# A fused attention and MoE kernel: batch 0 in two query parts (384, 192) with a MoE span for each, and a new order of the early loads

## The chip, the cores and the metric

The kernel runs on one core of one Trainium2 chip. The metric is the device time of one execution in microseconds (us). A profile gives the span from the first to the last instruction, some 2 us less. The experiments ran in four sets of rounds on four chips, each with the kernel before beside it. Engines: PE does the matmuls, DVE is VectorE, ACT is ScalarE, POOL is GpSimd (it also issues the DMAs that cast from fp32 to bf16), SP issues the plain DMAs.

## The reference

Block-causal attention over q, k, v of 8 batches x 8 heads x 576 tokens x 64, blocks of 64; then a maxout MoE on the 4608 rows of 512:

```python
scores = q @ k.T / sqrt(64)        # masked where block_i < block_j
attn   = softmax(scores);  x = (attn @ v) as rows of 8*64
out    = maximum(x @ w1, x @ w2) @ w_out     # 512 -> 1024 -> 512
```

## The kernel before

Heads go in pairs, four a batch, 32 in all. For a pair, `burst_a` and `burst_b` compute transposed scores and exponentials into a packed tile `aT`; `av` multiplies with v (a column of ones gives the sum); `x_out` transposes the result into `xT`, from which the MoE matmuls read. All matmuls stand in one fixed PE order:

```python
    def burst_a(p):
        ...                            # keys of chunk 0, 0 and 1
        exp(p, u0, 512, 0); mask(p, 0)
        exp(p, u1, 512, 512); mask(p, 576)
    def burst_b(p):
        ...                            # chunks 2 and 3, then 4
        exp(p, u2, 512, 1024); mask(p, 1024); mask(p, 1344)
        exp(p, u3, 64, 1536, m=BLK)
    ...
    for s in range(HP):                # batch 0: attention alone
        burst_a(s)
        ...                            # casts, transposes, warm_up dummies, av(0)
        burst_b(s)
        pool_work(s)                   # POOL: casts and requests of loads
    for p in (1, 2, 3):
        av(p, [0, 1]); av(p, [2, 3, 4])
        if p == 2: x_out(0)
    x_out(1)                           # only now is MoE work ready
    for s in range(HP, NPAIR):         # pairs 4 to 31
        n = fill_of(s)                 # MoE matmuls to lay beside this pair
        burst_a(s); fill(n_a); ...; burst_b(s); ...; av(s - 2); fill(...)
```

`fill(n)` emits the next n matmuls of the MoE, which goes in nine spans of 512 tokens: `h_unit` (4 + 4 matmuls for 128 hidden columns, one eviction to `h1` and one maximum, both on DVE) and `y_unit` (8 matmuls, one eviction on ACT, one store). A span may start when its tokens are done; batch 0 gives 576, so one span.

The softmax here doesn't subtract the row's maximum and nothing guards it: scores larger than these inputs give would overflow.

Of the kernel before, what the change touches and what calls it, by code (L numbers as in the profile page):

```python
# [14 lines left out]
def kernel(  # L15
# [38 lines left out]

    SPAN = 512
    NSPAN = NTOK // SPAN

# [31 lines left out]
    def load_qk(g, queues, gated=False):  # L89
        b, u = divmod(g, GPB)  # L90
        for nm, src, queue in (("q", q, queues[0]), ("k", k, queues[1])):
            raws[nm, g] = t = raw.tile([P, 2, RPP * D], FP32, name=f"{nm}raw")
            if gated:
                nc.gpsimd.memset(t[:, 0, :1], 0.0)
            queue.dma_start(
                out=t[:],
                in_=src[b, 4 * u:4 * u + 4].rearrange(
                    "(s h) (p t) d -> (h p) s (t d)", h=2, t=RPP),
            )
# [35 lines left out]
    load_qk(2, (SP, SP))  # L135
# [9 lines left out]
    cast("q", 0, ((dve, 0, 6), (pool, 6, RPP)))  # L145
# [3 lines left out]
    cast("q", 1, ((pool, 0, RPP),))  # L149
    for c in range(3, NCH):  # L150
        load_v(0, c)
    load_w(0, 256)
    load_w(256, 256)
# [5 lines left out]
    def h_unit(i, f):  # L159
        if f == 0:  # L160
            g_tiles[i] = g_pool.tile([P, NFF, SPAN], BF16, name="g")
        g = g_tiles[i]
        t0 = i * SPAN
        ph = []
        for w_sb in (w1_sb, w2_sb):
            pt = ps_m.tile([P, SPAN], FP32, name="ps_h", tag="m")
            for c in range(NDM):
                nc.tensor.matmul(  # L168
                    pt[:], w_sb[:, c, f * P:(f + 1) * P], xT[:, c, t0:t0 + SPAN],
                    start=(c == 0), stop=(c == NDM - 1),  # L170
                )
                if c == NDM - 1:
                    if not ph:
                        h1 = h1_pool.tile([P, SPAN], BF16, name="h1")
                        nc.vector.tensor_copy(out=h1[:], in_=pt[:])  # L175
                    else:
                        nc.vector.tensor_max(g[:, f, :], h1[:], pt[:])  # L177
                    ph.append(pt)
                yield

    def y_unit(i, s):
        g = g_tiles[i]
        t0 = i * SPAN + s * P
        py = ps_m.tile([P, d_model], FP32, name="ps_y", tag="m")
        for f in range(NFF):
            nc.tensor.matmul(  # L186
                py[:], g[:, f, s * P:(s + 1) * P], wo_sb[:, f, :],
                start=(f == 0), stop=(f == NFF - 1),
            )
            if f == NFF - 1:  # L190
                y = y_pool.tile([P, d_model], FP32, name="y")
                nc.scalar.copy(out=y[:], in_=py[:])  # L192
                nc.sync.dma_start(out=out[t0:t0 + P, :], in_=y[:])
            yield

    def y_last(i, s):
        g = g_tiles[i]
        t0 = i * SPAN + s * P
# [17 lines left out]
    def moe():  # L216
        ny = SPAN // P
        for i in range(NSPAN):
            need = (i + 1) * SPAN
            for f in range(NFF):  # L220
                yield from ((need, 0) for _ in h_unit(i, f))
                if i > 1 and f % 2 == 0:
                    yield from ((need, 0) for _ in y_unit(i - 1, f // 2))
            if i == 0:
                for s in range(ny):
                    yield from ((need, 0) for _ in y_unit(0, s))
        for s in range(ny - 1):
            yield from ((NTOK, 0) for _ in y_unit(NSPAN - 1, s))
        yield from ((NTOK, 0) for _ in y_last(NSPAN - 1, ny - 1))


    needs = []
    for i in range(NSPAN):
        needs += [(i + 1) * SPAN] * (2 * NDM * NFF + (SPAN // P * NFF if i != 1 else 0))
    needs += [NTOK] * ((SPAN // P + 1) * NFF)
    moe_steps = moe()
    at = [0]

    def ready():
        n = at[0]  # L240
        while n < len(needs) and needs[n] <= done_tokens[0]:
            n += 1
        return n - at[0]

    def fill(n):
        for _ in range(min(n, ready())):
            next(moe_steps)
            at[0] += 1
# [43 lines left out]
    def mask(p, a0):  # L292
        nc.gpsimd.memset(aT_r[p % NA][BLK:, :, a0:a0 + BLK], 0.0)  # L293
# [23 lines left out]
    def av(p, ts):  # L317
# [11 lines left out]
        for gi, t in enumerate(ts):  # L329
            for hh in range(2):  # L330
                for c in range(t + 1):
                    a0 = CB[c] + t * P
# [12 lines left out]
    def x_out(g):  # L345
        b, u = divmod(g, GPB)
        xp = xps.pop(g)
        pe = ps_m.tile([P, 2, NCH, BLK], BF16, name="ps_xe", tag="m")
        po = ps_m.tile([P, 2, NCH - 1, BLK], BF16, name="ps_xo", tag="m")
        for s in range(2):  # L350
            for t in range(NCH):
                src = xp[:, t, s].rearrange("p a d -> p (a d)")
                nc.tensor.transpose(pe[:, s, t, :], src[:BLK], ident[:BLK, :BLK])  # L353
                if t < NCH - 1:
                    nc.tensor.transpose(po[:, s, t, :], src[BLK:], ident[BLK:, BLK:])
        dst = xT[:, 2 * u:2 * u + 2, b * S:b * S + NCH * P].rearrange(
            "p s (t h w) -> p s t h w", h=2, w=BLK)
        nc.vector.tensor_copy(out=dst[:, :, :, 0], in_=pe[:])  # L358
        nc.vector.tensor_copy(out=dst[:, :, :NCH - 1, 1], in_=po[:])  # L359
        if u == GPB - 1:  # L360
            done_tokens[0] = (b + 1) * S
# [13 lines left out]
    def pool_work(s):  # L375
        g, i = divmod(s, 2)
        if s == 0:
            load_w(512, 512)
            load_qk(3, (SP, SP), gated=True)
        elif s == 1 or s == 2:  # L380
            pass
        elif s == 3:
            cast("q", 2, ((act, 0, RPP),))
            cast("k", 2, ((act, 0, RPP),))
            load_qk(4, (SP, SP), gated=True)
            for c in range(3):
                load_v(1, c)
            cast("q", 3, ((pool, 0, RPP),))
            cast("k", 3, ((pool, 0, RPP),))
            for c in range(3, NCH):  # L390
                load_v(1, c)
            load_wo(0, 4)
            load_wo(4, 4)
        elif s == 4:
# [25 lines left out]
    warm_up(3)  # L420
# [4 lines left out]
    for s in range(HP):  # L425
        burst_a(s)
        if s == 0:
            cast("k", 1, ((dve, 0, RPP),))
            warm_up(4)
        elif s == 1:  # L430
            transposes("k", 1, (dve, dve))()
            warm_up(2)
        elif s == 2:
            av(0, [0, 1])
            warm_up(2)
        else:
            av(0, [2, 3, 4])
        burst_b(s)
        pool_work(s)
        if s == 0:  # L440
            transposes("q", 1, (dve, dve))()
            warm_up(2)
        elif s == 1:
            warm_up(4)
        elif s == 2:
            warm_up(3)
    for p in (1, 2, 3):
        av(p, [0, 1])
        av(p, [2, 3, 4])
        if p == 2:  # L450
            x_out(0)
    x_out(1)

    x_due = []
    for s in range(HP, NPAIR):
        g, i = divmod(s, 2)
        if x_due:
            x_out(x_due.pop())
        n = fill_of(s)
        if s == HP:  # L460
            fill(6)
            cq = transposes("q", 2, (dve, act))
            ck = transposes("k", 2, (dve, act))
            cq()
            ck()
            fill(6)
# [8 lines left out]
        if s >= HP + LAG:  # L475
# [4 lines left out]
            if p % 2:  # L480
                x_due.append(p // 2)
        else:
# [10 lines left out]
    fill(len(needs))  # L493
# [36 lines left out]
```

## Time and profile before

| | before |
|---|---|
| time (median of 3; range) | 294.72 us (293.98 to 294.97); with the fourth run of the result's rounds 294.64 |
| span of the profile, granted clock | 292.3 us, 0.998 |
| PE busy; DVE; ACT; POOL | 96%; 62%; 48%; 33% |
| first MoE matmul | 27.1 us |
| scores of pair 4, of pair 5 | 32.0, 36.7 us |
| DMA engines | nearly full from 2 to 46 us |

A busy PE is not a useful PE here, so the argument uses one count throughout, explained in the prediction: each matmul gets the time that it takes at its best, the dummies none, and "behind" is the time since the start less the useful time of all matmuls ahead of the current one. In the tables below I applied it in program order, so that the 1 to 2% of matmul records that six of the traces lack do not matter (the value at 28 us is then 19.7 us, against 19.5 in the prediction).

### The profile page before, as it was taken

The page shows a single profiled execution, that of the slowest core. Times are in us where ns is not written, and L with a number is a line of the kernel's source. Part 1 is how long each engine was busy: PE and PEld are TensorE (multiplying, and loading weights), DVE is VectorE, ACT ScalarE, POOL GpSimd, SP SyncE. Part 2 cuts the span into 40 slices and gives each one's busy share as a digit, 9 for nine tenths or more (in the row PEclk, how much of TensorE's full clock was granted, in tenths as well). Part 3 has the DMA queues.
Part 4 walks back from the last instruction along what each step waited for, and adds up shares of the span by engine and source line. Part 5 has one row for each costly group of instructions (what it writes and reads, how often), then busy time and mean ns, then how long its engine had stood idle before and what let it go on. Part 6 is the DMA issues. An engine that isn't in the chain of part 4 may idle for free.

```text
span 292.3 us, 7455 instructions
## 1 busy us (share of the span) xinstructions
PE 281.2 (96%) x3116; PEld 141.0 (48%) x3116; DVE 181.9 (62%) x363; ACT 140.2 (48%) x200; POOL 95.7 (33%) x236
## 2 busy tenths in 40 slices
PE   8787999999999999999999999999999999999995
PEld 3345445445554454544454455454545544444443
DVE  6717677547986676666565656666665766464530
ACT  3883686686655555554545555545555000101112
POOL 2967536625644443144324532443111000000000
PEclk9999999999999999999999999999999999999999
DMA  7999999968923792568656594465110111011104
GB/s 265 288 182 295 224 183 172 234 150 166 200 34 142 97 212 46 199 73 201 82 200 72 116 168 153 76 61 65 40 38 37 38 69 41 36 72 38 72 36 144
DMA packets 56081, 36.65 MB, mean 125 GB/s; under 512 B 38768, under 2 KB 43376, under 8 KB 56048
## 3 DMA queue, kind: packets, MB, share of 16 engines
q0 software_dynamic: 41728, 7.87, 34.5%
q1 hardware_dynamic: 13760, 27.60, 27.8%
q10 hardware_dynamic: 560, 0.72, 0.7%
q8 instruction: 24, 0.39, 0.6%
q14 instruction: 9, 0.07, 0.1%
HBM read 34.60 MB, written 9.44 MB: 151 GB/s over the span
## 4 chain that ended last, share of the span: by engine, by line
PE 89%; ACT 4%; DVE 3%; DMA 2%; issue 1%; ACTq 0%
PE ps_h L168 43%; PE ps_y L186 20%; PE ps_o L333 11%; PE ps_s L282 8%; ACT aT L288 3%; PE ps_qT L265 2%; DMA qraw<-in_q_dram 2%; PE ps_kT L265 2%; PE ps_xe L353 2%; PE ps_w L254 1%; DVE xp L340 1%; PE ps_y L203 1%; DVE xT L358 0%; DVE qT L272 0%; DVE kT L272 0%
## 5 line engine op out<-in xcount | busy, mean ns | idle before, releaser
L168 PE MATMUL ps_h<-xT,w_sb 128*128 128x512 bf16 x576 | 139.6, 380 | 0.5 <-DVE xT L359 0.4
L288 ACT ACTIVATE aT<-ps_s 128x1024 bf16<-128x1024 f32 (+1 forms) x128 | 99.2, 832 | 53.5 <-PE ps_s L282 53.5
L168 PEld LDWEIGHTS <-w_sb 128*128 128x128 bf16 x576 | 51.8, 98 | 59.7 <-issue 6.1
L175 DVE CAST h<-ps_h 128x512 bf16<-128x512 f32 x72 | 49.7, 691 | 45.0 <-PE ps_h L168 43.9
L186 PE MATMUL ps_y<-wo_sb,g 128*128 128x512 bf16 x280 | 69.6, 379 | 0.0
L293 POOL MEMSET aT<- 64x128 bf16 x128 | 23.6, 200 | 120.7 <-ACT aT L288 120.5
L192 ACT COPY y<-ps_y 128x512 f32<-128x512 f32 x35 | 20.5, 587 | 83.9 <-PE ps_y L186 61.4
L177 DVE TENSOR_TENSOR g<-h,ps_h 128x512 bf16<-128x512 bf16 x72 | 49.3, 684 | 10.2 <-PE ps_h L168 10.2
L333 PEld LDWEIGHTS <-aT 128*128 128x128 bf16 x960 | 33.6, 98 | 14.9 <-DVE xp L340 8.4
L333 PE MATMUL ps_o<-vv,aT 128*128 128x65 bf16 x960 | 39.7, 194 | 0.9 <-DVE xp L340 0.4
L186 PEld LDWEIGHTS <-g 128*128 128x128 bf16 x280 | 25.4, 98 | 27.9 <-issue 3.2
L282 PE MATMUL ps_s<-qT,kT 64*128 64x64 bf16 (+4 forms) x384 | 34.5, 275 | 3.0 <-ACT aT L288 2.9
L109 POOL DMA_DIRECT2D vv<-in_v_dram x40 | 33.7, 848 | 0.3 <-issue 0.3
L340 DVE TENSOR_TENSOR xp<-ps_o,rec 128x256 bf16<-128x256 f32 x64 | 31.4, 491 | 2.2
L282 PEld LDWEIGHTS <-kT 64*128 64x128 bf16 x384 | 16.5, 94 | 18.9 <-issue 13.2
L339 DVE RECIPROCAL rec<-ps_o 128x4 f32<-128x4 f32 x64 | 11.8, 184 | 18.9 <-PE ps_o L333 18.8
L105 POOL CAST qn<-qraw 128x1152 bf16<-128x1152 f32 (+1 forms) x15 | 17.1, 1138 | 4.8 <-DMA qraw<-in_q_dram 4.7
L272 DVE COPY qT<-ps_qT 128x576 bf16<-128x576 bf16 x17 | 12.8, 757 | 5.3 <-PE ps_qT L265 4.1
L358 DVE COPY xT<-ps_xe 128x640 bf16<-128x640 bf16 x16 | 7.8, 490 | 12.4 <-PE ps_xe L353 12.1
L105 POOL CAST kn<-kraw 128x1152 bf16<-128x1152 f32 x13 | 14.9, 1145 | 1.9 <-DMA kraw<-in_k_dram 1.2
L272 DVE COPY kT<-ps_kT 128x576 bf16<-128x576 bf16 x17 | 12.8, 756 | 4.3 <-PE ps_kT L265 3.3
L254 PE MATMUL ps_w<-zeros 128*128 128x512 bf16 x36 | 10.7, 432 | 1.7 <-DVE zeros L132 1.2
(39 smaller groups left out, 102.9 us busy)
## 6 DMA issues: line engine op xcount, KB each, us to landing
qraw<-in_q_dram SPq DMA_DIRECT2D x16, 576.0 KB, 4.4
out_dram<-y SPq DMA_DIRECT2D x35, 256.0 KB, 2.1
kraw<-in_k_dram SPq DMA_DIRECT2D x15, 576.0 KB, 6.5
vv<-in_v_dram POOLq DMA_DIRECT2D x32, 128.0 KB, 5.8
w_sb<-in_moe_w_dram POOLq DMA_DIRECT2D x4, 256.0 KB, 8.1
w_sb<-in_moe_w_dram POOLq DMA_DIRECT2D x2, 512.0 KB, 16.9
wo_sb<-in_moe_w_out_dram POOLq DMA_DIRECT2D x2, 512.0 KB, 12.6
kraw<-in_k_dram ACTq DMA_DIRECT2D x1, 576.0 KB, 5.6
```

What stands on the lines that cost most here:

```text
L105: copy(out=n[:, j0:j1], in_=t[:, j0:j1])
L109: nc.gpsimd.dma_start(out=vv_r[b % NV][:rows, c, :, :D], in_=v[b, :, c * P:c * P + rows, :].rearrange("h p d -> p h d"),)
L168: nc.tensor.matmul(pt[:], w_sb[:, c, f * P:(f + 1) * P], xT[:, c, t0:t0 + SPAN], start=(c == 0), stop=(c == NDM - 1),)
L175: nc.vector.tensor_copy(out=h1[:], in_=pt[:])
L177: nc.vector.tensor_max(g[:, f, :], h1[:], pt[:])
L186: nc.tensor.matmul(py[:], g[:, f, s * P:(s + 1) * P], wo_sb[:, f, :], start=(f == 0), stop=(f == NFF - 1),)
L272: copies[i](out=t[:, :S].rearrange("q (p j) -> q p j", j=RPP), in_=pts[i].rearrange("q j p -> q p j"),)
L282: nc.tensor.matmul(ps[:m, hh, col:col + w], kT[r, c * P:c * P + m], qT[r, q0:q0 + w], start=True, stop=True,)
L288: nc.scalar.activation(out=aT_r[p % NA][:m, :, a0:a0 + w], in_=ps[:m, :, :w], func=AF.Exp, scale=scale,)
L293: nc.gpsimd.memset(aT_r[p % NA][BLK:, :, a0:a0 + BLK], 0.0)
L333: nc.tensor.matmul(po[:, gi, hh, :], a[:, hh, a0:a0 + P], vv[:, c, h0 + 2 * hh, :], start=(mm == 0), stop=(mm == n_mm - 1),)
L340: nc.vector.tensor_mul(xp[:, ts[0]:ts[0] + n, :, p % 2], po[:, :, :, :D], rec[:, :n].to_broadcast([P, n, 2, D]),)
```

## The change

Its intent: let MoE matmuls start before batch 0's attention is complete. The first 384 queries of all four pairs go first; they need only the keys up to 384. Then a MoE span of 384 tokens can begin while the exponentials of the last 192 queries run. Spans become 384, 192, seven of 512 and 448, so 64 tokens of an output tile carry over from one span to the next. The diff, cut to its core:

```diff
-    NSPAN = NTOK // SPAN
+    spans = [(0, QCUT), (QCUT, S - QCUT)]                 # QCUT = 384
+    spans += [(t0, min(SPAN, NTOK - t0)) for t0 in range(S, NTOK, SPAN)]
+    carry = [t0 % P for t0, _ in spans]
...
+            if carry[i]:
+                nc.gpsimd.tensor_copy(out=g_tiles[i][:, :, :carry[i]], in_=...)
...
+    def burst_p1(p): burst(p, ((0, 0, QCUT), (2, 256, P)), 0)
+    def burst_p2(p): burst(p, ((1, P, QCUT - P),), 512)
+    def burst_q1(p): burst(p, ((0, QCUT, 192), (1, QCUT, 192), (2, QCUT, P)), 768)
+    def burst_q2(p): burst(p, ((2, 512, BLK), (3, QCUT, 192), (4, 512, BLK)), 1280)
...
-    for s in range(HP):
-        burst_a(s)
...
+    burst_p1(0); burst_p2(0); ...  # pairs 0 to 3, with av(p, [0, 1, 2]) between
+    load_w(0, 256); load_qk(2, (None, SP), gated=True)
...
+    burst_q1(2); transposes("q", 2, (dve, dve))(); fill(3); burst_q2(2); ...; fill(3)
+    burst_q1(3); transposes("k", 2, (dve, dve))(); av(0, [3, 4]); fill(3)
+    burst_q2(3); mask_q(3)
+    cast("q", 3, ((pool, 0, RPP),)); cast("k", 3, ((pool, 0, RPP),))
+    load_qk(4, (SP, SP), gated=True)
+    load_wo(0, 4); load_wo(4, 4)
+    fill(3); av(1, [3, 4]); fill(4)
```

The listing joins some lines with semicolons. q and k are loaded for two pairs at a time, a group: q4 and k4 are batch 2's first, q3 and k3 those of the group before. They were requested ahead of w_out before too (q4 at 22.9, w_out at 30.9 us in the old trace). In the new order they stand behind the two casts of q3 and k3.

More of the change, by code (lines that the diff above doesn't have):

```diff
@@ L53, with a_col @@
     NCH = 5
-    SPAN = 512
-    NSPAN = NTOK // SPAN
+    QCUT = 384
+    def a_col(p, c, t):
+        if p >= HP:
+            return CB[c] + t * P
+        return {
+            0: (0, 768 - QCUT), 1: (512 - P, 960 - QCUT),
+            2: (384 - 2 * P, 1152 - QCUT), 3: (0, 1344 - QCUT), 4: (0, 1536 - 4 * P),
+        }[c][t * P >= QCUT] + t * P if (c, t) != (2, 4) else 1280
+    SPAN = 512
+    spans = [(0, QCUT), (QCUT, S - QCUT)]
+    spans += [(t0, min(SPAN, NTOK - t0)) for t0 in range(S, NTOK, SPAN)]
+    NSPAN = len(spans)
+    carry = [t0 % P for t0, _ in spans]
+    tiles = [(carry[i] + w) // P for i, (_, w) in enumerate(spans)]
     wpool = ctx.enter_context(tc.tile_pool(name="wpool", bufs=1))
@@ L91, in load_qk @@
         for nm, src, queue in (("q", q, queues[0]), ("k", k, queues[1])):
+            if queue is None:
+                continue
             raws[nm, g] = t = raw.tile([P, 2, RPP * D], FP32, name=f"{nm}raw")
@@ L134 @@
     load_qk(1, (SP, SP))
-    load_qk(2, (SP, SP))
+    load_qk(2, (SP, None))
     make_identity(nc, ident)
@@ L144 @@
         nc.vector.memset(aT_r[r][:BLK, :, AW:], 0.0)
-    cast("q", 0, ((dve, 0, 6), (pool, 6, RPP)))
+    cast("q", 0, ((dve, 0, 7), (pool, 7, RPP)))
     cast("k", 0, ((act, 0, 5), (dve, 5, RPP)))
@@ L148 @@
         load_v(0, c)
-    cast("q", 1, ((pool, 0, RPP),))
-    for c in range(3, NCH):
-        load_v(0, c)
-    load_w(0, 256)
-    load_w(256, 256)
+    cast("k", 1, ((pool, 0, RPP),))
     done_tokens = [0]
@@ L160, in h_unit @@
         if f == 0:
-            g_tiles[i] = g_pool.tile([P, NFF, SPAN], BF16, name="g")
+            g_tiles[i] = g_pool.tile([P, NFF, SPAN + BLK], BF16, name="g")
+            if carry[i]:
+                end = carry[i - 1] + spans[i - 1][1]
+                nc.gpsimd.tensor_copy(
+                    out=g_tiles[i][:, :, :carry[i]],
+                    in_=g_tiles[i - 1][:, :, end - carry[i]:end])
         g = g_tiles[i]
-        t0 = i * SPAN
+        t0, w = spans[i]
+        m = carry[i]
         ph = []
@@ L168, in h_unit @@
                 nc.tensor.matmul(
-                    pt[:], w_sb[:, c, f * P:(f + 1) * P], xT[:, c, t0:t0 + SPAN],
+                    pt[:, :w], w_sb[:, c, f * P:(f + 1) * P], xT[:, c, t0:t0 + w],
                     start=(c == 0), stop=(c == NDM - 1),
@@ L174, in h_unit @@
                         h1 = h1_pool.tile([P, SPAN], BF16, name="h1")
-                        nc.vector.tensor_copy(out=h1[:], in_=pt[:])
+                        nc.vector.tensor_copy(out=h1[:, :w], in_=pt[:, :w])
                     else:
-                        nc.vector.tensor_max(g[:, f, :], h1[:], pt[:])
+                        nc.vector.tensor_max(g[:, f, m:m + w], h1[:, :w], pt[:, :w])
                     ph.append(pt)
@@ L182, in y_unit @@
         g = g_tiles[i]
-        t0 = i * SPAN + s * P
+        t0 = spans[i][0] - carry[i] + s * P
         py = ps_m.tile([P, d_model], FP32, name="ps_y", tag="m")
@@ L197, in y_last @@
         g = g_tiles[i]
-        t0 = i * SPAN + s * P
+        t0 = spans[i][0] - carry[i] + s * P
         w = d_model // 2
@@ L214, in y_last, with plan, h, y @@
                 yield
-    def moe():
-        ny = SPAN // P
+    units = []
+    def plan():
+        def h(i, f):
+            t0, w = spans[i]
+            units.append((h_unit(i, f), t0 + w, w / SPAN, 2 * NDM))
+        def y(i, s, last=False):
+            t0, w = spans[i]
+            if last:
+                units.append((y_last(i, s), t0 + w, 0.5, 2 * NFF))
+            else:
+                units.append((y_unit(i, s), t0 + w, 1.0, NFF))
         for i in range(NSPAN):
-            need = (i + 1) * SPAN
             for f in range(NFF):
-                yield from ((need, 0) for _ in h_unit(i, f))
-                if i > 1 and f % 2 == 0:
-                    yield from ((need, 0) for _ in y_unit(i - 1, f // 2))
-            if i == 0:
-                for s in range(ny):
-                    yield from ((need, 0) for _ in y_unit(0, s))
-        for s in range(ny - 1):
-            yield from ((NTOK, 0) for _ in y_unit(NSPAN - 1, s))
-        yield from ((NTOK, 0) for _ in y_last(NSPAN - 1, ny - 1))
-    needs = []
-    for i in range(NSPAN):
-        needs += [(i + 1) * SPAN] * (2 * NDM * NFF + (SPAN // P * NFF if i != 1 else 0))
-    needs += [NTOK] * ((SPAN // P + 1) * NFF)
-    moe_steps = moe()
+                h(i, f)
+                if i > 2 and f % 2 == 0 and f // 2 < tiles[i - 1]:
+                    y(i - 1, f // 2)
+            if i == 1:
+                for j in range(2):
+                    for s in range(tiles[j]):
+                        y(j, s)
+        n = tiles[-1]
+        for s in range(n):
+            y(NSPAN - 1, s, s == n - 1)
+    plan()
+    steps = [(u, need, cost) for u, need, cost, n in units for _ in range(n)]
     at = [0]
     def ready():
-        n = at[0]
-        while n < len(needs) and needs[n] <= done_tokens[0]:
+        n, total = at[0], 0.0
+        while n < len(steps) and steps[n][1] <= done_tokens[0]:
+            total += steps[n][2]
             n += 1
-        return n - at[0]
+        return int(total)
     def fill(n):
-        for _ in range(min(n, ready())):
-            next(moe_steps)
+        while n > 0 and at[0] < len(steps) and steps[at[0]][1] <= done_tokens[0]:
+            u, _, cost = steps[at[0]]
+            next(u)
+            n -= cost
             at[0] += 1
@@ L290, in exp, with mask, burst, burst_p1 @@
         )
-    def mask(p, a0):
-        nc.gpsimd.memset(aT_r[p % NA][BLK:, :, a0:a0 + BLK], 0.0)
+    def mask(p, a0, eng=None):
+        (eng or nc.gpsimd).memset(aT_r[p % NA][BLK:, :, a0:a0 + BLK], 0.0)
+    def burst(p, parts, a0):
+        u = ps_s.tile([P, 2, 512], FP32, name="ps_s", tag="s")
+        w = 0
+        for c, q0, n in parts:
+            scores(p, u, w, c, q0, n)
+            w += n
+        exp(p, u, w, a0)
+    def burst_p1(p):
+        burst(p, ((0, 0, QCUT), (2, 256, P)), 0)
+    def burst_p2(p):
+        burst(p, ((1, P, QCUT - P),), 512)
+    def burst_q1(p):
+        burst(p, ((0, QCUT, 192), (1, QCUT, 192), (2, QCUT, P)), 768)
+    def burst_q2(p):
+        burst(p, ((2, 512, BLK), (3, QCUT, 192), (4, 512, BLK)), 1280)
+    def masks_p(p, eng=None):
+        for a in (0, 384, 512):
+            mask(p, a, eng)
+    def mask_q(p, eng=None):
+        mask(p, 1344, eng)
     def burst_a(p):
@@ L331, in av @@
                 for c in range(t + 1):
-                    a0 = CB[c] + t * P
+                    a0 = a_col(p, c, t)
                     nc.tensor.matmul(
@@ L343, in av, with x_out @@
         )
-    def x_out(g):
+    def x_out(g, t0=0, t1=NCH):
         b, u = divmod(g, GPB)
-        xp = xps.pop(g)
-        pe = ps_m.tile([P, 2, NCH, BLK], BF16, name="ps_xe", tag="m")
-        po = ps_m.tile([P, 2, NCH - 1, BLK], BF16, name="ps_xo", tag="m")
+        xp = xps[g]
+        n = t1 - t0
+        n_odd = min(t1, NCH - 1) - t0
+        pe = ps_m.tile([P, 2, n, BLK], BF16, name="ps_xe", tag="m")
+        po = ps_m.tile([P, 2, n_odd, BLK], BF16, name="ps_xo", tag="m")
         for s in range(2):
-            for t in range(NCH):
+            for t in range(t0, t1):
                 src = xp[:, t, s].rearrange("p a d -> p (a d)")
-                nc.tensor.transpose(pe[:, s, t, :], src[:BLK], ident[:BLK, :BLK])
+                nc.tensor.transpose(pe[:, s, t - t0, :], src[:BLK], ident[:BLK, :BLK])
                 if t < NCH - 1:
-                    nc.tensor.transpose(po[:, s, t, :], src[BLK:], ident[BLK:, BLK:])
-        dst = xT[:, 2 * u:2 * u + 2, b * S:b * S + NCH * P].rearrange(
+                    nc.tensor.transpose(po[:, s, t - t0, :], src[BLK:], ident[BLK:, BLK:])
+        dst = xT[:, 2 * u:2 * u + 2, b * S + t0 * P:b * S + t1 * P].rearrange(
             "p s (t h w) -> p s t h w", h=2, w=BLK)
         nc.vector.tensor_copy(out=dst[:, :, :, 0], in_=pe[:])
-        nc.vector.tensor_copy(out=dst[:, :, :NCH - 1, 1], in_=po[:])
+        nc.vector.tensor_copy(out=dst[:, :, :n_odd, 1], in_=po[:])
         if u == GPB - 1:
-            done_tokens[0] = (b + 1) * S
+            done_tokens[0] = min(b * S + t1 * P, (b + 1) * S)
     LAG = 2
@@ L376, in pool_work @@
         g, i = divmod(s, 2)
-        if s == 0:
-            load_w(512, 512)
-            load_qk(3, (SP, SP), gated=True)
-        elif s == 1 or s == 2:
-            pass
-        elif s == 3:
-            cast("q", 2, ((act, 0, RPP),))
-            cast("k", 2, ((act, 0, RPP),))
-            load_qk(4, (SP, SP), gated=True)
-            for c in range(3):
-                load_v(1, c)
-            cast("q", 3, ((pool, 0, RPP),))
-            cast("k", 3, ((pool, 0, RPP),))
-            for c in range(3, NCH):
-                load_v(1, c)
-            load_wo(0, 4)
-            load_wo(4, 4)
-        elif s == 4:
+        if s == 4:
             pass
@@ L419 @@
     ck = transposes("k", 0, (act, dve))
-    warm_up(3)
     cq((0,))
@@ L424 @@
     ck((1,))
-    for s in range(HP):
-        burst_a(s)
-        if s == 0:
-            cast("k", 1, ((dve, 0, RPP),))
-            warm_up(4)
-        elif s == 1:
-            transposes("k", 1, (dve, dve))()
-            warm_up(2)
-        elif s == 2:
-            av(0, [0, 1])
-            warm_up(2)
-        else:
-            av(0, [2, 3, 4])
-        burst_b(s)
-        pool_work(s)
-        if s == 0:
-            transposes("q", 1, (dve, dve))()
-            warm_up(2)
-        elif s == 1:
-            warm_up(4)
-        elif s == 2:
-            warm_up(3)
-    for p in (1, 2, 3):
-        av(p, [0, 1])
-        av(p, [2, 3, 4])
-        if p == 2:
-            x_out(0)
-    x_out(1)
-    x_due = []
+    cast("q", 1, ((dve, 0, RPP),))
+    burst_p1(0)
+    burst_p2(0)
+    warm_up(2)
+    masks_p(0)
+    load_w(0, 256)
+    load_qk(2, (None, SP), gated=True)
+    cq = transposes("q", 1, (dve, dve))
+    burst_p1(1)
+    ck = transposes("k", 1, (dve, dve))
+    for i in range(2):
+        cq((i,))
+        ck((i,))
+    burst_p2(1)
+    masks_p(1)
+    for c in range(3, NCH):
+        load_v(0, c)
+    warm_up(2)
+    burst_p1(2)
+    warm_up(2)
+    av(0, [0, 1, 2])
+    burst_p2(2)
+    masks_p(2, nc.vector)
+    load_w(256, 256)
+    warm_up(3)
+    burst_p1(3)
+    av(1, [0, 1, 2])
+    warm_up(2)
+    burst_p2(3)
+    masks_p(3, nc.vector)
+    load_w(512, 512)
+    load_qk(3, (SP, SP), gated=True)
+    cast("q", 2, ((pool, 0, RPP),))
+    cast("k", 2, ((pool, 0, RPP),))
+    burst_q1(0)
+    av(2, [0, 1, 2])
+    warm_up(2)
+    burst_q2(0)
+    av(3, [0, 1, 2])
+    x_out(0, 0, 3)
+    burst_q1(1)
+    warm_up(2)
+    burst_q2(1)
+    x_out(1, 0, 3)
+    mask_q(0)
+    mask_q(1)
+    for c in range(3):
+        load_v(1, c)
+    warm_up(1)
+    burst_q1(2)
+    transposes("q", 2, (dve, dve))()
+    fill(3)
+    burst_q2(2)
+    mask_q(2)
+    for c in range(3, NCH):
+        load_v(1, c)
+    fill(3)
+    burst_q1(3)
+    transposes("k", 2, (dve, dve))()
+    av(0, [3, 4])
+    fill(3)
+    burst_q2(3)
+    mask_q(3)
+    cast("q", 3, ((pool, 0, RPP),))
+    cast("k", 3, ((pool, 0, RPP),))
+    load_qk(4, (SP, SP), gated=True)
+    load_wo(0, 4)
+    load_wo(4, 4)
+    fill(3)
+    av(1, [3, 4])
+    fill(4)
+    x_due = [0]
     for s in range(HP, NPAIR):
@@ L457 @@
         if x_due:
-            x_out(x_due.pop())
+            x_out(x_due.pop(), 3 if s < HP + 2 else 0)
         n = fill_of(s)
-        if s == HP:
-            fill(6)
-            cq = transposes("q", 2, (dve, act))
-            ck = transposes("k", 2, (dve, act))
-            cq()
-            ck()
-            fill(6)
         burst_a(s)
@@ L481 @@
                 x_due.append(p // 2)
+        elif s == HP:
+            av(2, [3, 4])
+            fill(n_b)
+            av(3, [3, 4])
+            x_due.append(1)
         else:
@@ L492 @@
     x_out(NG - 1)
-    fill(len(needs))
+    fill(len(steps))
 _INS = ['q', 'k', 'v', 'moe_w1', 'moe_w2', 'moe_w_out']
```

## The prediction

> **What bounds the kernel now.** I read the page's slices first, then the chain of waits, then TensorE's and ScalarE's timelines of the first 60 us, and the landing time of each early DMA. TensorE (PE) is busy nearly everywhere:
>
> ```profile
> span 292.3 us, 7455 instructions
> ...
> PE   8787999999999999999999999999999999999995
> ...
> DMA  7999999968923792568656594465110111011104
> ...
> PE 89%; ACT 4%; DVE 3%; DMA 2%; issue 1%; ACTq 0%
> ```
>
> But the first four slices (29 us) are filled in part by dummy matmuls on zeros (L254, 36 of them). Batch 0's attention is paced by ScalarE's exponentials there; no MoE matmul exists before its whole 576 tokens are normalised and transposed. The timelines show it:
>
> ```profile
> 9.23 3.00 ACT L288 ACTIVATE aT<-ps_s 128x1024 bf16<-128x1024 f32 x4 [0.46 <-PE ps_s L282]
> 12.59 3.00 ACT L288 ACTIVATE aT<-ps_s 128x1024 bf16<-128x1024 f32 x4 [0.36 <-PE ps_s L282]
> 16.12 3.00 ACT L288 ACTIVATE aT<-ps_s 128x1024 bf16<-128x1024 f32 x4 [0.53 <-PE ps_s L282]
> 19.46 3.00 ACT L288 ACTIVATE aT<-ps_s 128x1024 bf16<-128x1024 f32 x4 [0.34 <-PE ps_s L282]
> ...
> 29.60 0.64 ACT L272 COPY qT<-ps_qT 128x576 bf16<-128x576 bf16 x1 [5.06 <-PE ps_qT L265]
> ```
>
> Four pairs of heads cost 13.2 us (9.23 to 22.46), of which 12.0 are exponentials. Then ScalarE stands for 5 us while PE, DVE and PE again finish the attention:
>
> ```profile
> 27.11 0.60 PE L168 MATMUL ps_h<-xT,w_sb 128*128 128x512 bf16 x2
> 28.09 1.02 PE L168 MATMUL ps_h<-xT,w_sb 128*128 128x512 bf16 x4 [0.38 <-DVE xT L359]
> ...
> 32.04 0.61 PE L282 MATMUL ps_s<-qT,kT 64*128 64x512 bf16 x6
> ...
> 36.65 0.61 PE L282 MATMUL ps_s<-qT,kT 64*128 64x512 bf16 x6
> ...
> 280.25 1.89 PE L168 MATMUL ps_h<-xT,w_sb 128*128 128x512 bf16 x8
> ```
>
> The first MoE matmul starts at 27.1, the scores of pair 4 at 32.0 and of pair 5 at 36.7. From about 237 us to the end there is MoE alone, one 512-column matmul every 0.216 us. So every us by which useful PE work moves forward at the start is a us at the end, unless it is lost again in between.
>
> I counted PE's useful time from the starts: 0.4215 ns a column for MoE, half of that for scores (two run side by side), 29 ns for each 65-column matmul, 14 to 20 ns a transpose, nothing for the dummies. By this count PE is 19.5 us behind an ideal engine at 28 us, 21 at 36, 24.4 at 60, then loses some 0.07 us per us while attention lasts (37.3 at 240) and nothing until about 280. The first 28 us are therefore the one large hole, and part of it (8.8 us until q and k are loaded, cast and transposed) can't go.
>
> **What the Trainium skill says.** "TensorE: Matmul & The Clock Gate", Back-to-back issue gap, gives N/2.4 + 2.5 ns for an isolated matmul of N columns: 216 ns at 512, 162 at 384, 82 at 192. It adds that real streams can differ; here the most common gap of the 512-column matmuls is 216, so I use it. Splitting 576 columns in two costs only 2.5 ns more per weight tile. "DMA: Bandwidth & Descriptors", Issuing engines are not separate DMA queues, says that all queues share the same 16 engines and interleave; the trace agrees: between 20 and 33 us the software queue (v, weights) moved about 90 KB per us while q and k were in flight, and about 185 alone, in bytes as written. "Perfetto Trace Analysis", Identifying the Most-Contended Engine, warns that busy PE is no measure of closeness to its peak; the 36 dummies and the 19.5 us behind a busy-looking row agree.
>
> **The change part by part.** *Queries split 384 and 192.* Exponentials stay four a pair (1024, 512, 1024, 640 elements a partition instead of 1024 three times and 128). With 0.975 us for 1024 and about 0.9 ns an element, a pair is 3.1 us against 3.0: no saving in itself. What is gained is order. I follow the in-order queues with durations of the old trace:
> - q0's cast is better split (POOL 256 columns instead of 384, which took 0.89) and the three dummies before the scores go: first exponential 8.8 instead of 9.23.
> - Group 1's q is now cast by DVE after its copies: 8.7 + 1.35 = 10.1; its transposes stand before pair 1's scores, which wait for them: ScalarE idle 0.4 us.
> - Pair 0's first value product stands ahead of pair 2's second scores. It needs v chunk 2, which landed at 15.5. One k load (1.45 us) now comes after it, so I take 14.4: the PE queue stands until 14.7, ScalarE idle about 1.5.
> - Then 1.5 us a half pair: the part of 384 queries is through the exponentials at 17.5, x_out of its second group at 20.6, xT written at 21.3, and the first MoE matmul starts at about 21.7, 5.4 earlier.
> - Up to pair 4 the fills are 3+3+3+3+4 units (a unit is one matmul of 512 columns, so one of 384 costs 0.75), which is 4+4+4+4+6 = 22 matmuls of 384, 0.162 us each: 3.6 us, laid between the remaining exponentials. Batch 1's first transposes lie there too. So pair 4's scores start at 28.05 instead of 32.04.
> - Stage of pair 4: the planner hands out just 5 units (7 matmuls), so it is bound by the four exponentials and the leftover value products: 4.6 us. Pair 5's scores start at 32.7 instead of 36.65: 3.95 earlier.
> - By then the old kernel has done 2+4+6+7+8 = 27 matmuls of 512 (13,824 columns), the new one 29 of 384 (11,136). The 2,688 columns missing are 1.1 us. All else due by then is done in both. **Net 2.8 us.**
>
> *Spans 384, 192, seven of 512, 448.* Total columns are unchanged. 64 more matmuls at 2.5 ns are 0.2 us. VectorE gets 16 more evictions and, with 192 columns, 8 matmuls last 0.7 us of PE while two evictions last about 0.55 (0.69 at 512, scaled with a small fixed part); with batch 1's copies beside them VectorE can hold PE up in that span: 0.3 to 0.8 us lost. Eight carry copies on POOL (64 tokens x 8) are off the path.
>
> *Loads.* w2's columns 512 to 1023 landed at 35.1 and were needed at 38. Now they are needed (matmul 36) at about 33.9. Before, batch 2's q and k were issued at 22.9 and shared the engines with them; now they are issued after q3's and k3's casts, about 27.5, so this load should be done by 32 to 33. w_out lands by about 45 as before; y of batch 0 starts near 48. Both margins are small and positive.
>
> Sum: 2.8 - 0.2 - 0.5, plus some 0.8 us that I expect back between 40 and 60 us, where the old kernel lost 3.5 and the new has 15 units a pair rather than 13 to fill it with: **2.9 us, 294.7 to 291.8.**
>
> **Rivals.**
> (a) *The weight load becomes the wait.* MoE starts 5.4 us earlier but the DMA engines are full from 2 to 46 us and the bytes are the same. If w2's second half still lands at 35.1, PE stands 1.2 us and everything behind it in the queue too; a late v chunk at 13 us adds up to 1. Against it: the order of issue. Time then 293 to 294.5.
> (b) *The start is better than I count.* If v comes in time and ScalarE has few gaps, batch 0 ends 2 to 3 us earlier: about 289. The bound is 8.8 + 4 x 3.1 = 21.3 for the last exponential, against about 26 that I get; but matmuls filled in between make the difference useful in part.
> (c) *Hidden anyway.* If the fill used early is missing in pairs 5 to 9, they become bound by ScalarE and the gain is given back before 62 us: about 294. Against it: 576 tokens are ready instead of 512, so the supply is larger by one eighth.
>
> **Range and chances.** My start may be off by 1.5 us either way, the two loads cost 0 to 1.5, (b) gives up to 3. 8 in 10: 288.9 to 294.6. Two per cent faster is 288.8, which needs (b) nearly whole: 0.12. Slower than 300.6 would need a hole of 9 us that nothing shows: 0.02.
>
> **What would show it.** Right: first ps_h matmul at 21 to 22.5, pair 4's first scores near 28, pair 5's near 32.7, useful PE work 2.5 to 3 us ahead at 60 us, and an unchanged saturated tail. Wrong: idle PE before ps_o near 13 us of over 2 us (v late), before ps_h near 33 us (w2 late) or before ps_y near 48 us (w_out late); VectorE above 90% in the span of 192; a first ps_h before 20 us would mean (b). A granted clock below 1.00 in the first 25 us, where 32 dummies instead of 36 keep PE busy, would break the durations that I used.

## The result, and the profile after

The changed kernel took 291.35 us (median of 4, 290.92 to 292.19) against 294.64 for the kernel before: ratio 0.9894, 95% interval 0.9866 to 0.9923. (A ratio is the mean time of one kernel's fast runs over that of the other's of the same rounds, so not quite the ratio of the medians.) The forecast was 291.8. The page after, its span, slices and chain by engine:

```profile
span 289.4 us, 7674 instructions
...
PE   7799989999999999999999999999999999999995
...
DMA  7999999969933792569366593366201011111114
...
PE 88%; DMA 4%; issue 2%; DVE 2%; ACT 2%; POOL 1%; ACTq 0%; POOLq 0%; DVEq 0%
```

The page's shares say little: PE rose by a point, while in the chain DMA rose from 2% to 4% and POOL entered with 1%. The ScalarE timeline after answers to the four blocks of exponentials before (start, duration, engine, line, tiles, shape, count, idle time ahead and what ended it):

```profile
8.95 1.51 ACT L324 ACTIVATE aT<-ps_s 128x1024 bf16<-128x1024 f32 x2
10.88 1.51 ACT L324 ACTIVATE aT<-ps_s 128x1024 bf16<-128x1024 f32 x2 [0.42 <-PE ps_s L318]
12.57 1.02 ACT L324 ACTIVATE aT<-ps_s 128x1024 bf16<-128x1024 f32 x1 [0.18 <-PE ps_s L318]
14.26 0.60 ACT L324 ACTIVATE aT<-ps_s 128x512 bf16<-128x512 f32 x1 [0.67 <-PE ps_s L318]
15.34 3.37 ACT L324 ACTIVATE aT<-ps_s 128x1024 bf16<-128x1024 f32 x4 [0.48 <-PE ps_s L318]
```

Half a pair takes 1.5 us, and the first gaps (0.42; 0.18 and 0.67) stand where the prediction put them. Then PE's timeline, the milestones and the waits:

```profile
13.72 0.28 PE L396 MATMUL ps_o<-vv,aT 128*128 128x65 bf16 x4 [0.41 <-DMA vv<-in_v_dram]
...
20.75 0.82 PE L191 MATMUL ps_h<-xT,w_sb 128*128 128x384 bf16 x4
...
27.15 0.59 PE L318 MATMUL ps_s<-qT,kT 64*128 64x512 bf16 x5
...
31.91 0.59 PE L318 MATMUL ps_s<-qT,kT 64*128 64x512 bf16 x5
...
37.39 1.80 PE L191 MATMUL ps_h<-xT,w_sb 128*128 128x384 bf16 x10
40.12 0.44 PE L301 MATMUL ps_qT<-ident,qn 64*128 64x64 bf16 x18 [0.93 <-POOL qn L126]
...
47.12 0.81 PE L191 MATMUL ps_h<-xT,w_sb 128*128 128x192 bf16 x5 [0.22 <-DVE kT L308]
```

The first MoE matmul starts at 20.75 us instead of 27.11, pair 4's scores at 27.1 instead of 32.0, pair 5's at 31.9 instead of 36.7. Two places are new: PE stands for 0.93 us before the transposes of q4, and the span of 192 has gaps. In that span VectorE's timeline shows the two evictions of a unit:

```profile
43.05 0.35 DVE L198 CAST h<-ps_h 128x192 bf16<-128x192 f32 x1
43.50 0.35 DVE L200 TENSOR_TENSOR g<-h,ps_h 128x192 bf16<-128x192 bf16 x1
```

Behind in us, old and new:

| at | 20 | 28 | 36 | 44 | 52 | 60 | 80 | 240 us |
|---|---|---|---|---|---|---|---|---|
| before | 15.6 | 19.7 | 20.9 | 21.7 | 22.8 | 24.4 | 26.3 | 37.6 |
| after | 14.8 | 16.1 | 17.6 | 19.2 | 21.2 | 22.1 | 23.4 | 34.7 |
| gain | 0.8 | 3.6 | 3.3 | 2.5 | 1.6 | 2.3 | 2.9 | 2.9 |

3.6 us are won by 28 us, 2.0 are given back between 28 and 52, 1.3 return by 80, and from there nothing changes: 292.3 - 289.4 = 2.9.

### The profile page after: what moved, and what is told of

Its sections match the earlier page's. It is cut to its first block, busy times and chain, and to the rows that moved or that the text cites. A ratio compares the mean times of both kernels' runs of the same rounds, so it can differ in the third digit from the quotient of the medians.

```text
span 289.4 us, 7674 instructions
## 1 busy us (share of the span) xinstructions
PE 280.3 (97%) x3200; PEld 145.2 (50%) x3200; DVE 186.2 (64%) x391; ACT 137.8 (48%) x196; POOL 101.2 (35%) x241
## 3 DMA queue, kind: packets, MB, share of 16 engines
q0 software_dynamic: 41728, 7.87, 33.8%
q1 hardware_dynamic: 13760, 27.60, 28.2%
## 4 chain that ended last, share of the span: by engine, by line
PE 88%; DMA 4%; issue 2%; DVE 2%; ACT 2%; POOL 1%; ACTq 0%; POOLq 0%; DVEq 0%
PE ps_h L191 41%; PE ps_y L209 21%; PE ps_o L396 12%; PE ps_s L318 8%; DMA vv<-in_v_dram 2%; PE ps_xe L418 2%; DMA qraw<-in_q_dram 2%; PE ps_qT L301 2%; PE ps_kT L301 1%; ACT aT L324 1%; PE ps_w L290 1%; DVE xp L403 1%; POOL vv L130 1%; PE ps_y L226 1%; POOL qn L126 1%
## 5 line engine op out<-in xcount | busy, mean ns | idle before, releaser
L191 PE MATMUL ps_h<-xT,w_sb 128*128 128x512 bf16 (+3 forms) x640 | 140.7, 358 | 0.4 <-DVE kT L308 0.2
L324 ACT ACTIVATE aT<-ps_s 128x1024 bf16<-128x1024 f32 (+3 forms) x128 | 100.1, 832 | 60.4 <-PE ps_s L318 58.5
L191 PEld LDWEIGHTS <-w_sb 128*128 128x128 bf16 x640 | 56.8, 98 | 57.1 <-issue 6.1
L198 DVE CAST h<-ps_h 128x512 bf16<-128x512 f32 (+3 forms) x80 | 50.9, 636 | 43.4 <-PE ps_h L191 41.2
L200 DVE TENSOR_TENSOR g<-h,ps_h 128x512 bf16<-128x512 bf16 (+3 forms) x80 | 50.6, 632 | 9.9 <-PE ps_h L191 7.6
L318 PE MATMUL ps_s<-qT,kT 64*128 64x64 bf16 (+6 forms) x408 | 34.7, 269 | 1.3 <-ACT kT L308 0.7
L403 DVE TENSOR_TENSOR xp<-ps_o,rec 128x256 bf16<-128x256 f32 (+1 forms) x64 | 31.4, 491 | 2.2
L402 DVE RECIPROCAL rec<-ps_o 128x4 f32<-128x4 f32 (+1 forms) x64 | 11.8, 185 | 14.6 <-PE ps_o L396 14.5
L181 POOL COPY g<-g 128x512 bf16<-128x512 bf16 x8 | 4.9, 614 | 37.9 <-DVE g L200 37.8
L423 DVE COPY xT<-ps_xe 128x640 bf16<-128x640 bf16 (+2 forms) x18 | 8.2, 453 | 11.9 <-PE ps_xe L418 11.4
```

Of the source, the lines that this page charges most:

```text
L191: nc.tensor.matmul(pt[:, :w], w_sb[:, c, f * P:(f + 1) * P], xT[:, c, t0:t0 + w], start=(c == 0), stop=(c == NDM - 1),)
L198: nc.vector.tensor_copy(out=h1[:, :w], in_=pt[:, :w])
L200: nc.vector.tensor_max(g[:, f, m:m + w], h1[:, :w], pt[:, :w])
L318: nc.tensor.matmul(ps[:m, hh, col:col + w], kT[r, c * P:c * P + m], qT[r, q0:q0 + w], start=True, stop=True,)
L324: nc.scalar.activation(out=aT_r[p % NA][:m, :, a0:a0 + w], in_=ps[:m, :, :w], func=AF.Exp, scale=scale,)
L403: nc.vector.tensor_mul(xp[:, ts[0]:ts[0] + n, :, p % 2], po[:, :, :, :D], rec[:, :n].to_broadcast([P, n, 2, D]),)
```

## The experiments

All are edits of the changed kernel, but for e4, and all gave the right result. Ratios are to the kernel before in the same rounds; the changed kernel has 0.9894.

**e1, e12: no MoE work before pair 4.** The five fills are taken out:

```diff
-    fill(3) ... fill(3) ... fill(3) ... fill(3) ... fill(4)
```

> The changed kernel without the 22 MoE matmuls laid between batch 0's last exponentials (the five fills ahead of pair 4 are gone, the two spans and the attention order stay). Theory A (the gain comes from MoE work done in PE's idle time there): pair 4's scores come some 2 us earlier than the 27.1 us of the changed kernel, but 3.6 us of matmuls are moved behind them, so the time rises by 1.2 to 2.2 us, to about 293. Theory B (the gain is the attention's own shorter chain, the fills only moved work about): the time stays within 0.5 us of 291.35. Theory C (all of the gain is the fills): 294.5 or more.

294.2 us (median of 6), ratio 0.9999 (0.9985 to 1.0013): **the whole gain is gone**, more than theory A's size and just short of C's. Its profiled run was its slowest (296.77 us), so I profiled the same kernel once more:

> The kernel of e1 once more for a profile, as e1's profiled run (296.77 us) was the slowest of its six (the others 294.06 to 294.90). Theory A (PE's idle time near 25 us lets the granted clock fall in every execution): the clock falls again and the time is 294 to 297. Theory B (only in some): the clock is 1.00 throughout, about 294.1, and pair 5's scores start some 2.5 us later than they would for the same work in the changed kernel.

295.05 us. PE's timeline and two stretches of e12 (duration, then busy us and instructions of PE, PEld, DVE, ACT and POOL, granted clock, DMA share, GB/s):

```profile
25.04 0.59 PE L318 MATMUL ps_s<-qT,kT 64*128 64x512 bf16 x5
...
27.93 0.44 PE L301 MATMUL ps_qT<-ident,qn 64*128 64x64 bf16 x18 [1.71 <-POOL qn L126]
```
```profile
24.00:28.00 4.00, 1.38 (x19) 0.66 (x21) 1.24 (x5) 1.94 (x2) 3.82 (x6) 1.00 1.14 281
28.00:32.00 4.00, 3.90 (x65) 2.72 (x66) 2.25 (x6) 1.70 (x3) 2.53 (x5) 0.59 1.69 186
```

Pair 4's scores do come 2.1 us earlier (25.0 against 27.1), as A said. But nothing is won by it there: PE then waits 1.7 us for the cast of q3, whose load has its own time. Between 24 and 28 us PE is busy 1.38 us, and in the next 4 us the granted clock is 0.59 (0.50 in e1's profile). The clock is not what loses the gain: by the same count e12 is already 3.3 us further behind than the changed kernel at 28 us, while the clock still reads 1.00, and five of e1's six runs show a mean clock of 0.998 to 1.0 (0.987 in the profiled one) and still took 294.06 to 294.9 us. So the clock falls in some executions only (theory B of e12), and the gain is gone without it. e12 is 38.4 us behind at 240 us, 3.7 more than the changed kernel; 22 matmuls of 0.162 are 3.6. So what the fills win is the use of idle PE time. Attention that is merely earlier meets a load.

**e4: the spans alone**, in the kernel before (its attention and loads kept):

```diff
-    NSPAN = NTOK // SPAN          # nine of 512
+    spans = [(0, 384), (384, 192)] + ...   # with carry and the new planner
```

> The kernel before with the new spans alone (384, 192, seven of 512, 448, with carry copies), attention and loads of batch 0 as before. Both first spans become ready together at 576 tokens. Theory A (narrow matmuls cost 0.2 us and hold VectorE for about 1 us in the span of 192, 64 more tokens ready early give little): 294.6 plus 0 to 1.5 us. Theory B (the extra supply of 64 tokens, not the earlier start, is what gains): 293 or less.

296.26 us, ratio 1.0074 (1.0058 to 1.0089): 2.2 us slower, more than A allowed; B falls. Against the kernel before it is 0.3 us further behind at 44, 1.0 at 52, 1.3 at 60 and 1.9 at 80, then constant. The step from 44 to 52 is the span of 192. The 0.6 us from 60 to 80 I did not track to one cause. So the spans are a price, and the rest of the change earns it back: some 5 us from e4 to the changed kernel (0.9894 over 1.0074 is 0.982). e1 stands between the two at 0.9999. By these ratios, and if the parts add, some 3 us of the 5 are the fills, and the other 2 are the new attention order and the new loads together. The loads alone, or the order alone, were not run.

**e2: q4 and k4 requested as early as their buffers are free.**

```diff
     mask_q(1)
+    load_qk(4, (SP, SP), gated=True)
...
     cast("k", 3, ((pool, 0, RPP),))
-    load_qk(4, (SP, SP), gated=True)
```

> The changed kernel with batch 2's first q and k requested as early as their buffers are free, about 21.9 us as in the kernel before (22.9), instead of 30.4. Theory A (two loads compete for full DMA engines): the 0.93 us for which PE waited at 39.2 for the cast of q4 is gone, but the second half of w2, which landed at 32.0, lands at 34 to 35.5 and PE waits 0.5 to 1.5 us in ps_h near 33.6; the time stays within 0.5 us of 291.35. Theory B (the order of requests doesn't matter to w2): the wait is gone and nothing takes its place, 290.3.

292.77 us (291.47 to 294.78), ratio 0.9959 (0.9927 to 0.9991). The wait for q4 went, and w2's second half landed at 35.9 instead of 31.9 (the expectations give landings of the changed kernel some 0.1 us late): theory A's exchange, but dearer than it said (a wait of 0.5 to 1.5 us, and a time within 0.5 us of 291.35). PE's timeline of e2, where the changed kernel has one run of 11 such matmuls in 1.96 us:

```profile
32.24 1.31 PE L191 MATMUL ps_h<-xT,w_sb 128*128 128x384 bf16 x7
35.90 0.82 PE L191 MATMUL ps_h<-xT,w_sb 128*128 128x384 bf16 x4 [2.35 <-DMA w_sb<-in_moe_w_dram]
...
37.31 3.55 PE L191 MATMUL ps_h<-xT,w_sb 128*128 128x384 bf16 x11
```

PE stood 2.35 us, and some 1.4 us later 11 matmuls took 3.55 us: 0.320 us each instead of 0.162. **In this execution a stall of two microseconds cost another 1.6 through the clock.** Two of e2's six runs, this one and the slowest, show a mean clock of 0.994; the four others show 0.998 to 1.0 and took 291.47 to 293.12 us.

**e3: w_out requested behind the cast of q4**, so that it can't share the engines with q4:

```diff
-    load_wo(0, 4); load_wo(4, 4)            # after load_qk(4)
+            load_wo(0, 4); load_wo(4, 4)    # beside pair 5, after cast("q", 4)
```

> The changed kernel with w_out requested behind the cast of q4 (about 36 us instead of 30.4). Theory A (q4 landed at 39.0 because w_out and v shared the engines with it): here w_out is in the queue behind v anyway until about 40, so q4 is helped little: it lands at 37.5 to 39 and 0 to 1 us is won. Theory B (w_out is what delays q4): q4 lands by 35.5, the 0.93 us wait is gone and the time is 290.3. In both w_out lands before y of batch 0 at 52; if it doesn't, PE waits in ps_y and the time rises.

291.61 us, ratio 0.991 (0.9895 to 0.9925). q4 landed at 38.5 us instead of 38.9 and the wait of 0.9 us stayed. Theory A: w_out does not delay q4. (The edit does a little more than it says: it also moves the request of q5 and k5 behind that cast, from 36.7 to 41.7 us. So all these together held q4 back by 0.4 us in these two profiles. Whether the loads of v hold it back was not tested.)

**e5: `h1` of the span of 192 evicted by ScalarE.**

```diff
-                        nc.vector.tensor_copy(out=h1[:, :w], in_=pt[:, :w])
+                        (act if w <= 192 else dve)(out=h1[:, :w], in_=pt[:, :w])
```

> The changed kernel with the first of the two evictions (h1) of the span of 192 on ScalarE instead of VectorE, 8 copies of about 0.3 us. Theory A (VectorE, at 81 per cent in that stage, held PE up for about 1.1 us between 46.6 and 50.7): those gaps shrink to under 0.5 us, ratio to the kernel before 0.985 to 0.988 (0.9894 for the changed kernel). Theory B (ScalarE's exponentials of 1 us delay the copies as much): no gain or a loss, 0.989 to 0.993.

292.84 us, ratio 0.9958 (0.9933 to 0.9983): worse than either theory allowed. PE's timeline of e5 shows the new waits:

```profile
45.98 0.41 PE L191 MATMUL ps_h<-xT,w_sb 128*128 128x192 bf16 x3 [0.60 <-ACT h L198]
...
49.18 0.89 PE L396 MATMUL ps_o<-vv,aT 128*128 128x65 bf16 x24 [0.75 <-ACT kT L308]
```

ScalarE was busy 49% of that stage in the changed kernel, but its instructions are 1 us exponentials in a fixed order. In e5 two of them run from 43.8 to 45.7 us, and the copies behind them, at 45.6, are what PE waits for. This says that ScalarE is the wrong helper. It does not prove how much VectorE cost.

**e6: 9 units beside pair 4 instead of 5.**

```diff
-        n = fill_of(s)
+        n = max(fill_of(s), 9) if s == HP else fill_of(s)
```

> The changed kernel with 9 units instead of 5 beside pair 4 (some 5 matmuls of 384 more there, fewer beside pairs 5 to 9). Theory A (PE stood 0.7 us in ps_s at 28.9 for the exponentials, for lack of fill): half of it is used, and pairs 5 to 9 have enough left: 0.3 to 0.6 us faster than the changed kernel, ratio 0.987 to 0.9885. Theory B: the matmuls reach w2's second half (landing 32.0) sooner and wait for it, or the later pairs starve as much: ratio 0.9885 to 0.992.

291.58 us, ratio 0.9915 (0.989 to 0.994), theory B. It was 0.4 us less behind at 36 us and level at 44: the matmuls had only moved, and the wait for q4's late cast (0.6 us here) remained.

**e7: q4 and k4 requested before the casts of group 3.**

```diff
     mask_q(3)
+    load_qk(4, (SP, SP), gated=True)
     cast("q", 3, ((pool, 0, RPP),)); cast("k", 3, ((pool, 0, RPP),))
-    load_qk(4, (SP, SP), gated=True)
```

> The changed kernel with q4 and k4 requested before the casts of group 3 instead of behind them: about 26.6 us instead of 30.4. Theory A (q4's late request behind a cast that waits for k3, and w2's transfer, make the two waits): q4 lands at 34 to 36, the wait of 0.93 us at 39.2 is gone, w2's second half lands at 32.5 to 34 where it is needed at 33.6, a wait of 0 to 0.5 us; ratio 0.985 to 0.988. Theory B (any earlier q4 costs w2 as much, as in e2 where PE waited 2.3 us for it): ratio 0.989 to 0.993.

291.1 us (290.43 to 292.18), ratio 0.9889 (0.986 to 0.9918), between the two theories. q4 landed at 34.6 and its wait is gone. The profile, of the slowest of the five runs, shows another wait, in PE's timeline:

```profile
27.88 0.50 PE L191 MATMUL ps_h<-xT,w_sb 128*128 128x384 bf16 x2 [1.20 <-DMA w_sb<-in_moe_w_dram]
...
35.27 0.82 PE L191 MATMUL ps_h<-xT,w_sb 128*128 128x384 bf16 x4 [0.22 <-DMA w_sb<-in_moe_w_dram]
```

The second wait is A's price, though w2's second half landed at 35.2 us, later than A said. The first is for w2's columns 256 to 511, which landed at 27.8 us here and at 25.9 in the changed kernel's profile. The edit's own request goes out at 27.2, too late to be the main cause: this landing differs between executions, from 22.7 us (e9) to 28.2 (e8), with the loads up to there requested in the same order.

**e8: no dummy matmuls after the first 16.**

```diff
-    warm_up(2) ... warm_up(3) ... warm_up(1)      # 16 matmuls in eight places
```

> The changed kernel without its 16 dummy matmuls after the first 16. Theory A (they hold the granted clock: in e1 and e2 it fell to 0.50 and 0.65 of full after PE had stood for some 2 us): the clock falls below 1.00 somewhere between 9 and 25 us, matmuls of 384 take twice 0.162 us there, ratio 0.992 or more. Theory B (they only delay the scores behind them): the clock stays at 1.00, the first ps_h comes 0.3 to 1 us earlier, ratio 0.985 to 0.989.

291.46 us, ratio 0.9908 (0.9882 to 0.9933). Stretches of e8:

```profile
12.00:16.00 4.00, 3.21 (x36) 1.99 (x37) 2.64 (x9) 2.84 (x5) 3.90 (x9) 0.53 1.21 134
16.00:20.00 4.00, 3.79 (x74) 2.74 (x72) 2.79 (x11) 3.08 (x5) 3.06 (x6) 0.62 1.45 229
```

A's mechanism holds: the clock fell to 0.53 and 0.62 (1.00 in the changed kernel). Its price does not: the first `ps_h` came at 21.2 us instead of 20.75, and the time can't be told from the changed kernel's. That stretch waits for other things. The dummies guard against little there. (The profiled run again had the late w2 columns, at 28.2 us, and a wait of 1.1 us.)

**e9: e7, and the last weight halves in pairs of 256 columns. e10: the changed kernel again, in the same rounds. e11: the split alone.**

```diff
-    load_w(512, 512)
+    load_w(512, 256)
+    load_w(768, 256)
```

> The changed kernel with q4 and k4 requested at about 27 us as in e7, and the last weight halves (512 columns each of w1 and w2) requested as two pairs of 256. Theory A (w2's second half is what an early q4 delays, and only its first 256 columns are needed at 33 to 35): the first pair lands by 32 and the second by 36, needed at about 37.5; neither the 0.93 us wait for q4 nor one for w2 is left, 0.5 to 1.2 us faster than the changed kernel. Theory B (executions differ by when the weight columns 256 to 511 land, and that decides): within 0.5 us of the changed kernel, with a spread of 1 to 1.5 us over its runs.

> The changed kernel itself, beside e9 on the same chip and once more with a profile. Ratio to the kernel before 0.987 to 0.992. Its runs spread by 1 us or more; if the profiled run is one of the slower ones, PE waits 1 to 1.5 us for w_sb at about 26.5 us, as the profiles of e7 and e8 show; if it is one of the faster ones, the columns 256 to 511 of w2 land at 26.0 or before and no such wait is there.

> The changed kernel with the last weight halves in two pairs of 256 columns, q4 and k4 requested where the changed kernel has them (30.4 us). Theory A (e9's millisecond-free gain of 1 us needs the earlier q4; the split only makes room for it): ratio 0.989 to 0.991, PE still waits 0.9 us or more for q4's cast near 39. Theory B (the split itself gains): 0.987 or less.

(The words "millisecond-free" in the last one are a slip and mean nothing.) e9: 290.37 us, five of six runs from 290.07 to 290.74 and one at 293.52; ratio 0.9884 (0.9845 to 0.9924). e10: 291.43 us, 291.27 to 291.67; ratio 0.9899 (0.9876 to 0.9922), with w2's columns at 25.6 us and no wait for them. e11: 291.84 us, ratio 0.9916 (0.9899 to 0.9933), its waits for casts 1.6 us in sum. In e9's profile no wait for a weight is left, and q4's is gone. PE's timeline of e9:

```profile
28.64 0.44 PE L301 MATMUL ps_qT<-ident,qn 64*128 64x64 bf16 x18 [0.36 <-POOL qn L126]
...
39.05 0.44 PE L301 MATMUL ps_qT<-ident,qn 64*128 64x64 bf16 x18
```

It is 18.3 us behind at 44, 0.9 less than the changed kernel. e11 shows that the split alone gains nothing (0.9916, just over theory A's 0.991, with A's wait for q4's cast). The traces suggest why the two edits belong together: with the early q4 w2's last columns land later (35.2 us in e7 against 31.9; 33.8 in e9 against 31.6 in e11), and the split makes only the first of them urgent. But by their times e7 (0.9889) and e9 (0.9884) can't be told apart, so that the split is needed beside the early q4 is not shown. By the medians e9 is the best version, 1.1 us under e10 (theory A's size), but one run in six was slow and the intervals overlap, so that it is faster is likely and not shown. The slow run has a mean clock of 0.994 (0.999 to 1.0 in the five others), as e2's profiled run with its long stall has; it was not profiled, so its cause stays open. e10's narrow spread did not bear out my expectation of 1 us.

## Why the prediction was right, point by point

- **The hole at the start.** Right: 3.6 us of PE time won by 28 us, by MoE matmuls laid into it; e1 takes just them away and loses everything.
- **The walk through the start.** First exponential 8.95 (predicted 8.8); ScalarE's gap for q1's transposes 0.42 (0.4); v's chunk landed at 13.7 (14.4), so that ScalarE's gap was 0.67 and not "about 1.5". From this, about 0.9 us of lead: first `ps_h` 20.75 (21.7), pair 4 at 27.1 (28.05), pair 5 at 31.9 (32.7). The 22 and 29 matmuls came as counted. The net at pair 5 is (36.65 - 31.9) - 1.1 = 3.7, not 2.8. This is in the direction of rival (b), a better start, but not its size: 0.9 us and not 2 to 3, and by the prediction's own sign (a first `ps_h` before 20 us) (b) did not come.
- **The weight as the new wait (rival a).** w2's second half landed at 31.9 (predicted 32 to 33), was needed at 33.6 (33.9), and PE did not wait. (In the old trace the matmul that needs it starts at 39.9, not at 38 as the prediction read it.) w_out landed at 48.5 and not by 45, but y started at 52.1 and not at 48. e2 shows how near it was: a request 8.5 us earlier, and PE waits 2.35 us. And in some executions w2's columns 256 to 511 come late, which I had not foreseen.
- **q4.** The prediction put its request at "about 27.5" and listed no wait for it. The cast of k3 ahead of it waited for k3, which landed at 29.1; so the request went out at 30.4, q4 landed at 38.9, and PE stood 0.93 us. e7 and e9, which move the request, remove the wait.
- **The span of 192.** 64 narrow matmuls at 83 ns (median start to start), as said. Five gaps between 46.6 and 50.7, beyond the best time, make 1.35 us, more than "0.3 to 0.8"; but the kernel before loses 1.1 us between 44 and 52 too, and e4, the spans alone, loses 0.7 more than it there, inside the range. The working had one size wrong: two evictions of 192 columns take 0.70 us (0.35 each; 0.55 each at 384 columns, 0.69 at 512) and not "about 0.55", so they last longer than the eight matmuls beside them (0.66). VectorE was at 81% of that stage, under the 90% that I had named as a sign. That VectorE makes the gaps fits this, but no run removed its load without adding another wait. In all, the spans alone cost e4 2.2 us and not the 0.7 of the sum; 1.2 of the 1.9 us that its profile shows by 80 us lie outside the stretch of 44 to 52, and their cause stays open.
- **"Some 0.8 us that I expect back between 40 and 60 us".** This did not come then: from 36 to 60 the new kernel lost 4.5 us and the old 3.5 (the prediction's 3.5 is for this stretch, not for 40 to 60). 0.8 of the 1.0 fell before 44, where q4's wait stands; from 44 on they lost 2.9 and 2.7. 0.6 us came back after 60. Rival (c) foresaw that some of the gain is given back, but not why: its mechanism, pairs bound by ScalarE, is not seen, as between 28 and 62 us PE waited for exponentials once, for 0.5 us (0.6 in the kernel before).
- **Sum.** Start 0.8 better than its term, middle worse by about as much; 2.9 predicted, 2.9 in the spans, 3.3 in the medians. The mechanism was right, but that the total fits so well is luck: two errors cancel.

In what it took from the Trainium skill: "TensorE: Matmul & The Clock Gate", Back-to-back issue gap, fits (83, 163, 189 and 216 ns measured as medians at 192, 384, 448 and 512 columns, against 82.5, 162.5, 189 and 216). "DMA: Bandwidth & Descriptors", Issuing engines are not separate DMA queues, fits as well: in e2, q4 and k4 on SP's queue delay a weight on POOL's by 4.0 us. The prediction's rates for the old trace are rough: read again, the software queue moved 101 KB per us from 20 to 33 us (92 to 96 from 24 on), and alone 143 to 196.

## What to carry to other kernels

Work of a later stage laid into the start pays by what it fills of the bound engine's idle time, so count useful time, not busy time, and expect earlier work to reach loads that were hidden. When DMA is full, look at which request stands behind which cast in the issuing engine's own order, and split a large load where only its first part is urgent. Before moving work from a loaded engine to an idle one, look at how long the instructions are that it would queue behind.

## What the Trainium skill lacked or had wrong

- "TensorE: Matmul & The Clock Gate", What's actually happening, lets the clock fall, by its table, after at least one idle window of about 3.4 us. In e2 one stall of 2.35 us, with PE busy on both sides, was followed by 3.5 us of matmuls at 320 ns instead of 162; stalls of 0.9 to 1.2 us (the changed kernel, e7) had no such effect. In e12 one of 1.04 and one of 1.71 us within 4 us were followed by a clock of 0.59. In e8 it fell after a stretch of 4 us (8 to 12) in which PE was still busy for 1.53.
- The same page, Back-to-back issue gap, gives about 131 ns for a sustained stream of 512-column matmuls. Here the median is 216 ns over 448 of them, its isolated figure.
- "DMA: Bandwidth & Descriptors", Queues, rings and completion order, tells how engines take turns between queues. No page says how far landings vary: w2's columns 256 to 511, requested between 15.2 and 15.6 us, landed at 22.7, 25.6, 25.9, 27.8 and 28.2 us in five profiles (e9, e10, changed, e7, e8).
